# Sparse attention with an ELU feed-forward: 64-bit weights decoded in pairs of pieces, where they are staged

## The chip, the cores and the metric

One core of one Trainium2 chip. The metric is the time of one execution on the device in microseconds, the median of several runs. TensorE (PE) multiplies matrices, VectorE (DVE) and ScalarE (ACT) do the elementwise work, GpSimd (POOL) some of it and the indirect DMAs, and SyncE (SP) issues most other DMAs. Each engine takes its instructions in a fixed order.

## The reference, cut to what matters

```python
# q, k, v: (4, 8, 768, 64) float32; blocks of 32 tokens, 24 of them
mask = |blk_i - blk_j| <= 1, or block 0 or 23 on either side, or one of 3 sampled blocks per row block
attn = softmax(where(mask, q @ k^T / 8, -1e9)) @ v
x = attn, tokens by 512                     # 3072 x 512
h = x @ w_in                                # w_in 512 x 2048, float64
g = where(h > 0, h, exp(min(h, 0)) - 1)
out = g @ w_out                             # w_out 2048 x 512, float64
```

The two weight matrices come as 64-bit floats. No engine here computes in them: the kernel takes them as two 32-bit words each and builds a 32-bit float from sign, exponent and mantissa bits, which it then splits into two 16-bit floats (high part and rest). All products are made of three 16-bit products (high by high, high by low, low by high).

## The kernel before

**The work.** The 3072 tokens are 12 chunks of 256, three for each of the 4 batches. A chunk has two units of 128 query rows. For each unit and each half of the heads (qd): scores on TensorE (`scores`, L459), their minimum on VectorE (`sm_min`, L471), exp on ScalarE (`sm_exp`, L486), P split into two halves (`sm_hi` L493, `sm_lo` L498), turned by a DMA transpose (`sm_T`, L505; in chunk 0's first two units by TensorE, `turn_p`, L354), and multiplied with V (`attn_v`, L518). V rows are gathered from a scratch tensor in DRAM (`gather_v`, L416 and L418; `edge_v`, L408), after they have been split and stored there (`store_v`, L398). The first and last block of queries see all keys; `special` (sp, spt, spp, L554 to L605) handles them. The result is normed (`norm`, L538) and turned (`turn_x`, L332) into `xT`, the chunk's input of the feed-forward part.

**Feed-forward.** For each chunk, 8 tiles of h (`ffn_h`, L634; 24 matmuls of 128x256 each, into one of three PSUM tiles "f"), for each of them exp and relu on ScalarE (L642, L648), the minimum with h on VectorE (L652, "e<-h,e", which frees the PSUM tile), the high part of g (L656) and its rest (L659, on VectorE in chunk 0, else on GpSimd). Then two output tiles (`ffn_o`, L670, in four parts each), which need every g and every part of w_out. They are copied out by L678.

**The weights.** w_in and w_out are 16 pieces each, of 128x512 64-bit values (512 KB). `load_w` reads a piece into a room: the first three into the ring `wk` of three rooms, the next four into the tiles of g, which are not needed yet, all others into `wk` again, once its room is free. `w_bits1` works in place on ScalarE: the high word is scaled so that its exponent field becomes that of a 32-bit float (L245), and the top three bits of the low word's mantissa are made an integer (L247). `w_bits2` builds the float in a new tile of the ring "e" by two operations of VectorE, each with two sources: sign or low bits (L256), then the high word shifted by three, or that (L258). `w_split` makes the high part on ScalarE (L267) and the rest on VectorE (L268), in four dictionaries of tiles (`wih`, `wil`, `woh`, `wol`). So a piece takes three operations of ScalarE and three of VectorE, each of 512 columns. The ring "e" has four tiles and is shared with the outputs of `norm`, the e tiles of the feed-forward part and the output tiles r.

**The order.** `Steps` is a list of functions by step and rank; chunk t's h starts at step 12 + 16 t. Piece i gets its first bits at step 2 + 2i/3 and the rest a step later, so all 32 fall into chunk 0's part. `gate` holds the decoding of pieces 3 and on behind exps of the first units, and `more_w` (L836) holds four loads behind the first unit's last V rows. From the list, a scheduler makes each engine's order and the waits.

Of the kernel before, what the change touches and what calls it, by code (L numbers as in the profile page):

```python
# [39 lines left out]
def kernel(  # L40
# [198 lines left out]

    def w_bits1(i):  # L240


        s = wst[i]
        u = s.bitcast(F32)[:, :, 1]
        first = nc.scalar.activation(u, u, AF.Copy, scale=2.0 ** -111)  # L245

        nc.scalar.activation(  # L247
            s[:, :, 0], s.rearrange("p e w -> p (e w)").bitcast(U16).rearrange("p (e w) -> p e w", w=4)[:, :, 1],
            AF.Copy, scale=2.0 ** -13, bias=2.0 ** -14 - 0.5)
        return first  # L250

    def w_bits2(i):
        s = wst.pop(i)
        x = work.tile([P, 512], I32, tag="e", bufs=NE, name=f"wx{i}")
        wx[i] = x
        nc.vector.scalar_tensor_tensor(  # L256
            x, s[:, :, 1], -(2 ** 31), s[:, :, 0], op0=ALU.bitwise_and, op1=ALU.bitwise_or)
        nc.vector.scalar_tensor_tensor(  # L258
            x, s[:, :, 1], 3, x, op0=ALU.logical_shift_left, op1=ALU.bitwise_or)

    def w_split(i):
        hi, lo, nm = (wih, wil, "wi") if i < NFC else (woh, wol, "wo")
        f = i % NFC
        hi[f] = const.tile([P, 512], F16, tag=f"{nm}h{f}", name=f"{nm}h{f}")
        lo[f] = const.tile([P, 512], F16, tag=f"{nm}l{f}", name=f"{nm}l{f}")
        x = wx.pop(i).bitcast(F32)
        nc.scalar.activation(hi[f], x, AF.Copy)  # L267
        nc.vector.tensor_tensor(lo[f], x, hi[f], op=ALU.subtract)  # L268
# [354 lines left out]
    gh = [gg[f // 2][:, 0, f % 2] for f in range(NFP)]  # L623
    gl = [gg[f // 2][:, 1, f % 2] for f in range(NFP)]

    def ffn_h(t, f):
        ps = ps_f.tile([P, 2, CW], F32, tag="f", name=f"h{t}_{f}")
        x = xT[t]
        for e in range(2):
            n = 0  # L630
            for cc in range(NCC):
                cs = slice(cc * P, (cc + 1) * P)
                for w, l in ((wih, 0), (wih, 1), (wil, 0)):
                    nc.tensor.matmul(  # L634
                        ps[:, e, :], lhsT=w[2 * f + e][:, cs], rhs=x[:, l, cc, :],
# [26 lines left out]
    def ffn_o(t, m, part, nparts):  # L662
# [4 lines left out]
        for f in range(NFP * part // nparts, NFP * (part + 1) // nparts):  # L667
            for e in range(2):
                for n, (g, w) in enumerate(((gh, woh), (gh, wol), (gl, woh))):
                    nc.tensor.matmul(  # L670
                        o, lhsT=g[f][:, e, ms], rhs=w[2 * f + e],
# [236 lines left out]
```

## Time and profile before

| what | value |
|---|---|
| median of 3 runs | 772.99 us (768.12 to 774.59) |
| the profiled execution's own time | 768.26 us |
| its span, first to last instruction | 766.5 us |
| busy: PE, DVE, ACT, POOL | 683.3, 461.8, 407.0, 194.1 us |
| mean granted TensorE clock | 0.95 |

A row of a group reads: line, engine, operation, output<-inputs, shapes, count | busy us, mean ns of one | idle time of the engine ahead of it and what ended it. A row of the timeline: start us, duration us, engine, line, operation, count [idle time ahead <-what ended it]. "issue" is idle time without a cause that the profile shows; SPq, DVEq are an engine's queue. The trace has 32 pieces decoded between 21.8 and 169 us.

### The profile page before, as it was taken

The numbers are of one execution on the slowest core, as the hardware profiler recorded it, in microseconds if no ns is written. First come the engines' busy times: TensorE is split into PE (matmuls) and PEld (weight loads), VectorE is DVE, ScalarE is ACT, GpSimd is POOL, SyncE is SP. The second block draws the span as 40 slices with busy tenths as digits, with TensorE's granted clock in tenths as the row PEclk, the third lists the DMA queues.
The fourth block names the chain that finished last, engine by engine and source line by source line (L and its number), as shares of the span: only waits on it lengthen the run. The fifth ranks groups of instructions, "written<-read, shape, count | busy, mean of one in ns | idle before, by whom it ended". The sixth has DMA issues, their size and how long they took to land. (4 is left out here: it accounts for less than half of the span.)

```text
span 766.5 us, 30298 instructions
## 1 busy us (share of the span) xinstructions
PE 683.3 (89%) x12999; PEld 476.1 (62%) x12999; DVE 461.8 (60%) x1253; ACT 407.0 (53%) x880; POOL 194.1 (25%) x193
## 2 busy tenths in 40 slices
PE   1447568599889999999999999999999999999997
PEld 1336454247646857758658658668568577586673
DVE  3849899686856755845655846647467358354130
ACT  2558798664834746545535546536456355353240
POOL 1414002001521421512413303325205215222040
PEclk9757789789999999999999999999999999999999
DMA  9996867969969678775796567597595635531000
GB/s 206 312 278 184 248 195 170 215 137 233 210 136 176 154 160 160 184 150 98 167 186 155 132 179 142 140 181 147 114 189 136 112 58 139 127 68 33 29 1 28
DMA packets 205307, 116.34 MB, mean 152 GB/s; under 512 B 163316, under 2 KB 183924, under 8 KB 205172
## 3 DMA queue, kind: packets, MB, share of 16 engines
q1 hardware_dynamic: 192464, 89.41, 53.6%
q0 software_dynamic: 5824, 17.83, 8.8%
q10 hardware_dynamic: 6884, 7.15, 3.4%
q8 instruction: 102, 1.67, 0.9%
q14 instruction: 33, 0.27, 0.1%
HBM read 74.52 MB, written 12.58 MB: 114 GB/s over the span
## 5 line engine op out<-in xcount | busy, mean ns | idle before, releaser
L634 PE MATMUL h<-xT,wih 128*128 128x256 f16 x1536 | 259.7, 276 | 7.5 <-DVE e L652 7.5
L670 PE MATMUL o<-woh,g 128*128 128x512 f16 x768 | 240.3, 384 | 3.7 <-ACT woh L267 3.7
L634 PE MATMUL h<-xT,wil 128*128 128x256 f16 x768 | 211.2, 275 | 0.0
L670 PEld LDWEIGHTS <-g 128*128 128x128 f16 x1152 | 109.9, 99 | 128.9 <-issue 5.1
L659 POOL TENSOR_TENSOR g<-e,g 128x512 f16<-128x512 f32 x88 | 102.9, 1172 | 322.0 <-DVE g L656 294.7
L634 PEld LDWEIGHTS <-wih 128*128 128x128 f16 x1536 | 148.1, 99 | 29.3 <-issue 6.6
L670 PE MATMUL o<-wol,g 128*128 128x512 f16 x384 | 146.9, 383 | 0.0
L418 POOL DMA_INDIRECT vg<-scr,rix x88 | 84.9, 964 | 204.2 <-PE av L518 183.7
L486 ACT ACTIVATE t<-t,m 128x256 f32<-128x256 f32 x176 | 87.2, 496 | 72.2 <-DVE m L471 72.2
L652 DVE SCALAR_TENSOR_TENSOR e<-h,e 128x512 f32<-128x512 f32 x96 | 66.1, 689 | 54.4 <-ACT e L648 51.3
L642 ACT ACTIVATE e<-h 128x512 f32<-128x512 f32 x96 | 56.3, 587 | 51.6 <-PE h L634 49.6
L634 PEld LDWEIGHTS <-wil 128*128 128x128 f16 x768 | 75.9, 99 | 9.8 <-issue 0.4
L471 DVE CUSTOM_DVE_ANT_1 t<-s,mask 128x256 f32<-128x256 f32 x176 | 64.6, 419 | 18.8 <-PE s L459 18.8
L498 DVE SCALAR_TENSOR_TENSOR p<-t,p 128x1024 f16<-128x1024 f32 x40 | 48.7, 1218 | 37.2 <-ACT p L493 37.2
L648 ACT ACTIVATE e<-e,gs 128x512 f32<-128x512 f32 x96 | 69.3, 722 | 1.8
L459 PEld LDWEIGHTS <-qT 64*32 64x32 f16 x4224 | 41.5, 93 | 41.6 <-issue 33.1
L459 PE MATMUL s<-kT,qT 64*32 64x96 f16 x2112 | 45.1, 214 | 16.4 <-issue 7.4
L459 PE MATMUL s<-kR,qT 64*32 64x160 f16 x2112 | 48.8, 245 | 11.9 <-DVE kR L427 5.3
L518 PEld LDWEIGHTS <-pT 128*32 128x32 f16 x4224 | 41.3, 96 | 21.1 <-issue 12.0
L518 PE MATMUL av<-vg,pT 128*32 128x64 f16 x4224 | 47.7, 198 | 6.9 <-DMA pT<-p 4.7
L427 DVE COPY kR<-kT 128x256 f16 x246 | 46.3, 235 | 10.4 <-issue 6.6
L656 DVE CAST g<-e 128x512 f16<-128x512 f32 x96 | 48.8, 508 | 2.7
(101 smaller groups left out, 635.1 us busy)
## 6 DMA issues: line engine op xcount, KB each, us to landing
vg<-scr SPq DMA_DIRECT2D x88, 192.0 KB
wk<-in_moe_w_out_dram SPq DMA_DIRECT2D x16, 512.0 KB
wk<-in_moe_w_in_dram SPq DMA_DIRECT2D x12, 512.0 KB
scr<-vN SPq DMA_DIRECT2D x12, 512.0 KB
out_dram<-r ACTq DMA_DIRECT2D x20, 256.0 KB
stq<-in_q_dram SPq DMA_DIRECT2D x18, 256.0 KB
stv<-in_v_dram SPq DMA_DIRECT2D x18, 256.0 KB
stk<-in_k_dram SPq DMA_DIRECT2D x18, 256.0 KB
```

What stands on the lines that cost most here:

```text
L418: nc.gpsimd.indirect_dma_start(out=t[0:96, 1, i], out_offset=None, in_=scr[b], in_offset=bass.IndirectOffsetOnAxis(ap=rix[0:96, qb : qb + ...
L459: nc.tensor.matmul(ps[32 * n : 32 * n + 32, j, pp, c], lhsT=qT[b, u][js, ql, a, q0 : q0 + 32], rhs=m, start=(ql + kl + part == 0), stop=(q ...
L471: nc.vector.tensor_tensor_reduce(t[:, j, pp, :].rearrange("p (a b) -> p a b", b=BLOCK), ps[:, j, pp, :].rearrange("p (a b) -> p a b", b=BL ...
L486: exps[b, u, qd] = nc.scalar.activation(t[:, j, pp, :], t[:, j, pp, :], AF.Exp, bias=m[:, j, pp : pp + 1], scale=-1.0, accum_out=s[:, h : ...
L518: nc.tensor.matmul(o[32 * n : 32 * n + 32, 4 * qd + 2 * pp + j, :], lhsT=t[:, pl * 8 + (2 * j + pp) * 2 + ab, 32 * n : 32 * n + 32], rhs=v ...
L634: nc.tensor.matmul(ps[:, e, :], lhsT=w[2 * f + e][:, cs], rhs=x[:, l, cc, :], start=(n == 0), stop=(n == 3 * NCC - 1))
L642: nc.scalar.activation(e, hS[t, f], AF.Exp, scale=IH)
L648: nc.scalar.activation(e, e, AF.Relu, bias=gs_col, scale=-GS)
L652: nc.vector.scalar_tensor_tensor(e, hS.pop((t, f)), -IH * GS, e, op0=ALU.mult, op1=ALU.min)
L656: nc.vector.tensor_copy(gh[f], eS[t, f])
L659: (nc.gpsimd if t else nc.vector).tensor_tensor(gl[f], eS.pop((t, f)), gh[f], op=ALU.subtract)
L670: nc.tensor.matmul(o, lhsT=g[f][:, e, ms], rhs=w[2 * f + e], start=(f == 0 and e == 0 and n == 0), stop=(f == NFP - 1 and e == 1 and n == 2))
```

## The change

1. **Pairs.** A table `WORK` lists 18 units of work in place of 32 pieces: 14 pairs of pieces, then four single pieces, each with its room. A pair is loaded by one DMA of 1 MB (w_in then in runs of 2 KB instead of 1 KB) and decoded by operations of 1024 columns.
2. **In place.** The float is built in the staged words themselves, in the word that was the low one, so every other word of the room holds a weight. The tile of the ring "e" goes.
3. **Sign.** Instead of L256 with two sources, an operation with one source (`tensor_scalar`, AND on 16-bit halves) puts the sign bit beside the integer of three bits, which ScalarE now writes as 16 bits. Then the shift and OR, in place. So a pair takes three operations of ScalarE and three of VectorE, as a single piece did.
4. **Rooms.** The weights' final tiles become `wi` (8) and `wo` (4), those of g two instead of four. A pair of w_in is staged in `wk`, in tiles of `wo` that wait for their weights, or in tiles of g; later ones in `wo` or `wk`.
5. **Loads.** Two pairs are asked for ahead of everything, two behind the first unit's V rows, three behind the second's; the others at the earliest step at which their room's last user is done, at most four steps ahead.

In `ffn_h` and `ffn_o` only the names of the tiles change; the matmuls are the same in number, shape and order within a tile.

```diff
+    WORK = [(0, 2, "k0"), (2, 2, 0), (4, 2, 1), (6, 2, 2), (8, 2, 3), (10, 2, "g0"),
...
+            (24, 2, 3), (26, 2, "k0"), (28, 1, "k2"), (29, 1, "k0"), (30, 1, "k1"), (31, 1, "k2")]
+    WFIRST, WMORE, WLATER = 2, 4, 7
...
     def w_bits1(i):
         s = wst[i]
-        u = s.bitcast(F32)[:, :, 1]
-        first = nc.scalar.activation(u, u, AF.Copy, scale=2.0 ** -111)
+        u, h = s.bitcast(F32)[:, :, 1], halves(s)
+        nc.scalar.activation(u, u, AF.Copy, scale=2.0 ** -111)
         nc.scalar.activation(
-            s[:, :, 0], s.rearrange("p e w -> p (e w)").bitcast(U16).rearrange("p (e w) -> p e w", w=4)[:, :, 1],
-            AF.Copy, scale=2.0 ** -13, bias=2.0 ** -14 - 0.5)
-        return first
+            h[:, :, 0], h[:, :, 1], AF.Copy, scale=2.0 ** -13, bias=2.0 ** -14 - 0.5)
+        nc.vector.tensor_scalar(h[:, :, 1], h[:, :, 3], 1 << 15, None, op0=ALU.bitwise_and)
 
     def w_bits2(i):
-        s = wst.pop(i)
-        x = work.tile([P, 512], I32, tag="e", bufs=NE, name=f"wx{i}")
-        wx[i] = x
-        nc.vector.scalar_tensor_tensor(
-            x, s[:, :, 1], -(2 ** 31), s[:, :, 0], op0=ALU.bitwise_and, op1=ALU.bitwise_or)
+        s = wst[i]
         nc.vector.scalar_tensor_tensor(
-            x, s[:, :, 1], 3, x, op0=ALU.logical_shift_left, op1=ALU.bitwise_or)
+            s[:, :, 0], s[:, :, 1], 3, s[:, :, 0], op0=ALU.logical_shift_left, op1=ALU.bitwise_or)
...
     def w_split(i):
...
+        x = wst.pop(i).bitcast(F32)[:, :, 0]
...
+        nc.scalar.activation(hi, x, AF.Copy)
+        nc.vector.tensor_tensor(lo, x, hi, op=ALU.subtract)
...
+    st.at(1, 9, lambda: more_w(0, range(WFIRST, WMORE)))
+    st.at(2, 9, lambda: more_w(1, range(WMORE, WLATER)))
+    for i, s in enumerate(w_step):
+        if i >= WLATER:
+            last = max((e for e in range(i) if held(e) & held(i)), default=0)
+            st.at(max(w_step[last] + 1, s - 4), 1.9, lambda i=i: load_w(i))
```

The scheduler's orders move with it, up to chunk 1's first h; from there on TensorE's order is the same. Three places. First VectorE, around chunk 0's first L652 (`e_0`; L671 in the changed kernel). Before (wx, wil: decoding; p, t, m: attention of unit 4):

```order
L256 SCALAR_TENSOR_TENSOR wx_1372<-wk 128x512
L323 SCALAR_TENSOR_TENSOR qT_5_1612<-qt_5_1613,qT_5_1612 128x512
L258 SCALAR_TENSOR_TENSOR wx_1372<-wk,wx_1372 128x512
L498 SCALAR_TENSOR_TENSOR p_4_0_1666<-t_4_0_1601,p_4_0_1666 128x1024
L268 TENSOR_TENSOR wil_1376<-wx_1372,wih_1375 128x512
L256 SCALAR_TENSOR_TENSOR wx_1411<-wk 128x512
L256 SCALAR_TENSOR_TENSOR wx_1414<-wk 128x512
L258 SCALAR_TENSOR_TENSOR wx_1411<-wk,wx_1411 128x512
L258 SCALAR_TENSOR_TENSOR wx_1414<-wk,wx_1414 128x512
L471 ISA t_4_1_1814,m_4_1_1815<-s_4_1_1673,mask 128x256
L471 ISA m_4_1_1815 128x1
L652 SCALAR_TENSOR_TENSOR e_0_1450<-h_0_1379,e_0_1450 128x512
```

In the changed kernel (L271 the AND, L275 shift and OR, L288 the rest):

```order
L271 TENSOR_SCALAR wo_87<-wo_87 128x1024
L343 SCALAR_TENSOR_TENSOR qT_4_1283<-qt_4_1284,qT_4_1283 128x512
L275 SCALAR_TENSOR_TENSOR wo_87<-wo_87 128x1024
L271 TENSOR_SCALAR wo_88<-wo_88 128x1024
L275 SCALAR_TENSOR_TENSOR wo_88<-wo_88 128x1024
L288 TENSOR_TENSOR wi_86<-wo_87,wi_86 128x1024
L671 SCALAR_TENSOR_TENSOR e_0_1355<-h_0_1297,e_0_1355 128x512
L671 SCALAR_TENSOR_TENSOR e_1_1485<-h_1_1330,e_1_1485 128x512
L675 CAST g_91<-e_0_1355 128x512
L288 TENSOR_TENSOR wo_87<-wo_88,wo_87 128x1024
L678 TENSOR_TENSOR g_91<-e_0_1355,g_91 128x512
L675 CAST g_91<-e_1_1485 128x512
```

The first two L652 now stand behind the last pair of w_in and ahead of all minima of unit 4, where they stood behind the first of that unit's two halves. With them TensorE's h0_3 and h0_4 have moved ahead of that unit's second scores.

Second SP, around the first DMA transpose of chunk 1's unit 4. Before:

```order
L416 DMA vg_85<-scr_221 96x1024 x2
L233 DMA wk<-in_moe_w_in_dram 128x4x256
L295 DMA stk_0_2078<-in_k_dram 128x8x64
L233 DMA wk<-in_moe_w_in_dram 128x4x256
L237 DMA wk<-in_moe_w_out_dram 128x1024 x2
L505 DMA_TRANSPOSE pT_4_0_1770<-p_4_0_1666 128x16x128
L237 DMA wk<-in_moe_w_out_dram 128x1024 x8
L505 DMA_TRANSPOSE pT_4_1_1927<-p_4_1_1908 128x16x128
```

In the changed kernel:

```order
L436 DMA vg_94<-scr_230 96x1024
L255 DMA wo_89<-in_moe_w_out_dram 128x2x1024
L436 DMA vg_94<-scr_230 96x1024
L255 DMA wo_90<-in_moe_w_out_dram 128x2x1024
L436 DMA vg_94<-scr_230 96x1024
L255 DMA wk<-in_moe_w_out_dram 128x2x1024
L436 DMA vg_94<-scr_230 96x1024
L333 DMA stq_2_1361<-in_q_dram 128x8x64
L255 DMA wk<-in_moe_w_out_dram 128x1024
L320 DMA stv_0_0_1701<-in_v_dram 128x4x128
L436 DMA vg_95<-scr_230 96x1024
L525 DMA_TRANSPOSE pT_4_0_1650<-p_4_0_1547 128x16x128
```

Ahead of the transpose all of w_in and four pairs and a single piece of w_out are asked for, where it was two pieces of w_out; the loads of pairs 9 and 10 (into wo_89, wo_90) stand among the V gathers of unit 4.

Third ScalarE, around the exps of the special rows (spt_1). Before:

```order
L267 ACTIVATE woh_2119<-wx_2113 128x512
L247 ACTIVATE wk<-wk 128x512
L267 ACTIVATE woh_2123<-wx_2116 128x512
L245 ACTIVATE wk<-wk 128x512
L247 ACTIVATE wk<-wk 128x512
L572 ACTIVATE spt_1_0_2163,spm_1_0_2160<-sp_1_0_2081,spm_1_0_2160 128x768
```

In the changed kernel (L267 and L269 are the bits, L287 the high part):

```order
L287 ACTIVATE wo_89<-wo_90 128x1024
L267 ACTIVATE wk<-wk 128x512
L269 ACTIVATE wk<-wk 128x512
L602 ACTIVATE spp_0_1_1926<-spt_0_1_1785,spm_0_1_1782 128x768
L592 ACTIVATE spt_1_0_2006,spm_1_0_2003<-sp_1_0_1934,spm_1_0_2003 128x768
L287 ACTIVATE wo_89<-wk 128x1024
```

The bits that stand ahead of these exps are now of a single piece in the ring's third room, which no piece used before it; it is asked for ahead of the transpose in the SP order above.

More of the change, by code (lines that the diff above doesn't have):

```diff
@@ L212, in build_mask @@
         nc.scalar.activation(mask, pm, AF.Copy, scale=NEG * SS)
-    gg = [const.tile([P, 2, 2, 2, CW], F16, tag=f"g{i}", name=f"g{i}") for i in range(NFP // 2)]
-    wih, wil, woh, wol, wst = {}, {}, {}, {}, {}
-    wx = {}
+    wi = [const.tile([P, 2, NCC, 2, P], F16, tag=f"wi{f}", name=f"wi{f}") for f in range(NFP)]
+    wo = [const.tile([P, 2, 2, 2, 512], F16, tag=f"wo{m}", name=f"wo{m}") for m in range(NFP // 2)]
+    gt = [const.tile([P, 2, 2, 2, 2, CW], F16, tag=f"g{i}", name=f"g{i}") for i in range(NFP // 4)]
@@ new lines @@
+    WFIRST, WMORE, WLATER = 2, 4, 7
+    assert NFC == 16
+    wst = {}
+    def w_room(i):
+        n, room = WORK[i][1:]
+        if room == "k0" and n == 2:
+            return wk[:, 0:2].rearrange("p a e w -> p (a e) w")
+        if str(room)[0] == "k":
+            return wk[:, int(room[1])]
+        x = gt[int(room[1])] if str(room)[0] == "g" else wo[room]
+        x = x.rearrange("p a b c d e -> p (a b c d e)" if str(room)[0] == "g" else "p a b c d -> p (a b c d)")
+        return x.bitcast(I32).rearrange("p (e w) -> p e w", w=2)
@@ L261, in w_split @@
     def w_split(i):
[L262 to L268, printed above, removed]
+        f, n, _ = WORK[i]
+        x = wst.pop(i).bitcast(F32)[:, :, 0]
+        if f < NFC:
+            hi, lo = (wi[f // 2][:, l].rearrange("p c e f -> p (c e f)") for l in range(2))
+        else:
+            f -= NFC
+            hi, lo = (wo[f // 4][:, f // 2 % 2, l, f % 2 : f % 2 + n].rearrange("p e d -> p (e d)")
+                      for l in range(2))
@@ L631, in ffn_h @@
             for cc in range(NCC):
-                cs = slice(cc * P, (cc + 1) * P)
-                for w, l in ((wih, 0), (wih, 1), (wil, 0)):
+                for xl, wl in PROD_X:
                     nc.tensor.matmul(
-                        ps[:, e, :], lhsT=w[2 * f + e][:, cs], rhs=x[:, l, cc, :],
+                        ps[:, e, :], lhsT=wi[f][:, wl, cc, e, :], rhs=x[:, xl, cc, :],
                         start=(n == 0), stop=(n == 3 * NCC - 1))
```

53 lines of the change are left out of this document (26 added, 27 removed).

## The prediction

> **What bounds the kernel now.** I read the stages first: the trace cut at the places where the work changes character. The columns are the stage, its length, then busy time of each engine with its number of instructions, the clock granted to TensorE, and the share of the DMA engines.
>
> ```profile
> core 0: us, PE busy (x) PEld busy (x) DVE busy (x) ACT busy (x) POOL busy (x), PEclk, DMA share, GB/s
> 24.00:60.00 36.00, 15.93 (x583) 12.33 (x570) 21.73 (x77) 19.25 (x48) 11.21 (x12) 0.55 0.99 269
> 60.00:120.00 60.00, 36.48 (x734) 28.69 (x722) 55.05 (x102) 51.52 (x111) 8.47 (x8) 0.78 0.72 211
> 120.00:177.00 57.00, 45.65 (x890) 25.26 (x890) 46.86 (x122) 38.28 (x81) 6.96 (x6) 0.85 0.84 190
> 177.00:766.00 589.00, 576.79 (x10776) 403.13 (x10774) 327.57 (x913) 288.75 (x627) 164.09 (x154) 1.00 0.61 132
> ```
>
> From 177 us on TensorE is busy 576.8 of 589 us at full clock: nothing but TensorE matters there, and whatever the start of that stage gains, the end gains. Ahead of it TensorE idles a third of the time. From 60 to 120 the full engine is VectorE (55.05 of 60), with ScalarE behind it (51.52); from 24 to 60 no engine is full, but DMA is (0.99).
>
> Next, the timeline of TensorE between 80 and 180 us, its idle times and what ended them (in brackets).
>
> ```profile
> 88.66 0.28 PE L459 MATMUL s<-kT,qT 64*32 64x96 f16 x8 [5.67 <-DVE m L471]
> ...
> 99.41 0.23 PE L518 MATMUL av<-vg,pT 128*32 128x64 f16 x1 [4.68 <-DMA pT<-p]
> ...
> 109.35 0.38 PE L634 MATMUL h<-xT,wih 128*128 128x256 f16 x2 [1.82 <-DVE e L652]
> ...
> 120.00 0.37 PE L634 MATMUL h<-xT,wih 128*128 128x256 f16 x1 [3.27 <-DVE e L652]
> ...
> 139.40 0.90 PE L332 MATMUL qt<-ident,stq 128*128 128x128 f32 x3 [5.35 <-ACT spt L572]
> ...
> 151.06 0.58 PE L670 MATMUL o<-woh,g 128*128 128x512 f16 x1 [3.66 <-ACT woh L267]
> ...
> 176.82 0.39 PE L634 MATMUL h<-xT,wih 128*128 128x256 f16 x2
> ```
>
> Three of these waits are for a VectorE operation (the minimum of the scores, then L652, which frees the PSUM tile of h) that stood in a full queue among weight pieces; the last wait is for a weight piece itself. The row at 176.82 is chunk 1's first h: the start of the stage that TensorE bounds. So the price of the change is how much earlier this row comes.
>
> The wait at 139.40 has its root on ScalarE, which sat in front of a w_out piece that had not landed, with the exps of the special rows behind it:
>
> ```profile
> 137.28 0.65 ACT L245 ACTIVATE wk<-wk 128x512 f32<-128x512 f32 x1 [5.70 <-DMA wk<-in_moe_w_out_dram]
> ```
>
> **The change, part by part.** First the prices. Groups with their mean duration in ns (last number ahead of the second bar), the two ring groups and the like of what comes in their place:
>
> ```profile
> L256 DVE SCALAR_TENSOR_TENSOR wx<-wk 128x512 int32<-128x512 int32 x28 | 18.9, 689 | 1.4 <-ACT wk L247 1.4
> L258 DVE SCALAR_TENSOR_TENSOR wx<-wk,wx 128x512 int32<-128x512 int32 x28 | 18.9, 687 | 0.0
> L268 DVE TENSOR_TENSOR wil<-wx,wih 128x512 f16<-128x512 f32 x16 | 10.9, 688 | 1.9 <-ACT wih L267 1.8
> L323 DVE SCALAR_TENSOR_TENSOR pT<-pt,pT 128x1024 f16<-128x1024 f32 x4 | 4.9, 1223 | 2.8 <-ACT pT L320 2.8
> L656 DVE CAST g<-e 128x512 f16<-128x512 f32 x5 | 2.1, 425 | 0.0
> L427 DVE COPY kR<-kT 128x256 f16 x246 | 46.3, 235 | 10.4 <-issue 6.6 <-PE s L459 1.6 <-PE pt L354 0.3
> L579 DVE TENSOR_SCALAR spm<-spm 128x1 f32<-128x1 f32 x16 | 2.5, 154 | 12.1 <-ACT spt L572 12.1
> ```
>
> and how closely such operations follow each other (start times in the first column):
>
> ```profile
> 60.09 1.23 DVE L323 SCALAR_TENSOR_TENSOR pT<-pt,pT 128x1024 f16<-128x1024 f32 x1 [1.47 <-ACT pT L320]
> 61.23 0.68 DVE L538 TENSOR_TENSOR xf<-av,sum 128x512 f32<-128x512 f32 x1
> 61.83 1.28 DVE L256 SCALAR_TENSOR_TENSOR wx<-g 128x512 int32<-128x512 int32 x2
> ...
> 110.42 0.42 DVE L656 CAST g<-e 128x512 f16<-128x512 f32 x1
> 110.75 0.69 DVE L258 SCALAR_TENSOR_TENSOR wx<-wk,wx 128x512 int32<-128x512 int32 x1
> ```
> ```profile
> 54.33 0.64 ACT L245 ACTIVATE g<-g 128x512 f32<-128x512 f32 x1
> 54.87 0.64 ACT L247 ACTIVATE g<-g 128x512 int32<-128x512 uint16 x1
> ...
> 91.55 1.05 ACT L493 ACTIVATE p<-t 128x1024 f16<-128x1024 f32 x1
> 92.49 0.68 ACT L245 ACTIVATE wk<-wk 128x512 f32<-128x512 f32 x1
> ```
>
> From start to start a two-source operation of 512 columns costs VectorE 0.60 us (61.23 to 61.83), one of 1024 costs 1.14 (60.09 to 61.23). ScalarE: 0.54 for 512, 0.94 for 1024. The new operation, the AND with one source, 1024 columns of 16 bit at every fourth place, has no row. A one-column operation takes 154 ns; the cast, one source at full width, adds (425 - 154)/512 = 0.53 ns a column; the copy of short runs of 16 bit (235 - 154)/256 = 0.32; two sources (1223 - 154)/1024 = 1.04. So the AND lies between 0.48 and 1.22 us. I take the cast's slope: 0.70 us, 0.61 from start to start.
>
> A pair of pieces thus costs VectorE 6 x 0.60 = 3.60 us before and 0.61 + 1.14 + 1.14 = 2.89 after; ScalarE 6 x 0.54 = 3.24 before and 3 x 0.94 = 2.82 after.
>
> *Term 1, from 60 us to L652 of the fifth h tile (h0_4), minus 11 us.* This is where VectorE is full.
>
> ```profile
> 60.00:119.25 59.25, 13.47 (x20) 0.78 0.72 208
> ```
> ```profile
> 119.25 0.69 DVE L652 SCALAR_TENSOR_TENSOR e<-h,e 128x512 f32<-128x512 f32 x1
> ```
>
> The first row is L256 alone in this stretch: 20 pieces, and L258 and L268 go with it, so 60 operations, 36.0 us of 59.25. In the change's order the same L652 has pairs 0 to 10 and two thirds of pair 11 ahead of it. Pairs 0 to 2 stand ahead of the last turned P of the first units, so they run before 60, where VectorE had 14 us to spare (21.73 of 36): one and a half pairs more than before are covered there. What is left is 8 x 2.89 + 1.75 = 24.9 us: 11.1 less. ScalarE has to follow: by the order it has 23 operations of 0.94 ahead of that point, 21.6 us, against about 60 of 0.54, 32.4, so it gives the same 11. TensorE has room for it (23.5 us idle in 60 to 120), and by the order h0_3 and h0_4 now stand ahead of the scores that waited 5.67 us.
>
> *Term 2, from there to 176.82, minus 6.5 us.* Decoding left: 9 pieces of 1.80 before, 16.2 us; after, 1.14 for pair 11, two pairs (5.8) and four single pieces of about 1.54 (6.2), 13.1. VectorE is busy 46.86 of 57 there, so I count half of the 3.1: 1.5. The wait of 5.70 goes: the piece that now stands ahead of those exps is read into a room that is free from the start. Singles 29 to 31 still reload used rooms, so 5 of it are counted. Bounds: 0 (another wait takes over at once) to 9.
>
> *Term 3, before 60, plus 4 us.* SP's queue now carries two loads of 1 MB ahead of the stores of vN and the V gathers, 0.5 MB more: at 269 GB/s 1.9 us later. The first product with V did not wait for V but for ScalarE, so most of this is covered; uncovered it is the 1.9.
>
> ```profile
> 41.37 0.71 PE L518 MATMUL av<-vg,pT 128*32 128x64 f16 x32 [1.11 <-ACT pT L320]
> ```
> ```profile
> PE s L459 <- issue: 11.7, 3, 4.9
> ```
> ```profile
> 21.78 0.71 ACT L245 ACTIVATE wk<-wk 128x512 f32<-128x512 f32 x1
> ```
>
> The third row is ScalarE's first decoding, without a wait; in the change it needs the whole megabyte, up to 1.9 us later, and the last split of K and those of Q stand behind it. For these two: 1.5. The second row: TensorE waited 11.7 us, in three pieces, all between 33 and 57 us, for nothing that the profile shows, in the stage with DMA at 0.99. The change brings 2 MB more forward by 60 us, 7.4 us more of such traffic; at 11.7 us per 36 that is 2.4 (0 to 6.5, if it lasts to 80).
>
> SP gets new waits: the loads of pairs 9 and 10 wait for the rooms of pairs 3 and 4, and the gathers of V for the fifth unit stand between and behind them. Both rooms come free ahead of the first h in VectorE's order; these V rows are first read at 99.41, three h tiles later. The transpose of P that follows on SP waits for VectorE anyway. I count nothing; if that cover were gone, the product at 99.41 would start later by the lateness of the gathers, as it now does by 4.68 for the transpose.
>
> Edits that cost nothing: the layout of w and g (same shapes and counts of matmuls and of stores), loads of w_in in runs of twice the length, the ring "e" without the decoded words.
>
> Sum: 768.26 - 11 - 6.5 + 4 = 754.8 for an execution like the profiled one. That one lies 4.7 under the median of the runs, 772.99; the four executions known (768.12 to 774.59) have a mean of 771.0, 2.7 above it. Forecast: 757.5, rounded **757 us**.
>
> **The rivals.**
> *A: the AND runs at one column per cycle of a two-source operation*, 1.22 us. For it: its columns lie 8 bytes apart, and no one-source row here is like that. Against: the cast. Price 0.53 us for each of 8.7 pairs in term 1 and about 1.5 behind: 6 us. 763.
>
> *B: the load moves to the front.* DMA at 0.72 from 60 to 120 leaves 28%, but pairs 4 to 8 are asked for in a burst, and if TensorE's unexplained waits go on until 80 us (6.5), and the 3.4 of loads ahead are not covered, term 3 is 10. For it: three waits in the full stage. Against: VectorE decodes on during them. 763 to 764.
>
> *C, slower: the writes to every other word.* The changed kernel's AND and shift write into the staged words, 8 bytes apart; before, VectorE read so but wrote dense (L256, L258). If such a write took two cycles a column, both would cost about 2.2 us, a pair 5.5, and term 1 would be 8.3 x 5.5 + 1.75 - 36 = +11 and the tail +7 instead of minus 1.5: about 784. It decides from about 1.5 ns a column for both operations on (there a pair costs 4.2 and term 1 is nothing). Against: L256 takes two sources so spaced at 689 ns, as much as L268 with dense ones (688).
> [...]
>
> *D: the attention chain binds, not VectorE's sum.* The wait of 4.68 for a DMA transpose stays as it is; if minimum, exp, transpose and product set the pace between 80 and 177, less decoding changes nothing: 768 to 771. Against: two waits for L652 and one for the minimum in the rows above, behind decoding.
>
> **How the numbers follow.** Main case 0.58 (745 to 764), A 0.10, B 0.18, C 0.06, D 0.08. Low end: the AND at 0.48 (3 us), term 2 at 9 and term 3 at 0: 745 after rounding. High end 770: D still in, C out. A measurement here tells about 1%, 7.7 us: below 763 is faster. Main 0.57, A 0.07, B 0.10 make 0.74; 0.18 within; slower is C and 0.02 of D, 0.08.
>
> **What would show it.** The AND near 0.70 us, the shift near 1.22; VectorE's time on decoding down from 66 us (96 operations of 0.69) to about 51; the fifth L652 at about 110 instead of 119.25; no wait for w_out ahead of the exps of the special rows; chunk 1's first h at about 163 instead of 176.82, and from there on the same length. Wrong: the AND or the shift above 1.5 us (C), waits on issue after 60 us (B), or an early fifth L652 and yet a late first h of chunk 1 (D).

## The result and the profile after

| kernel | median us | runs | ratio to before, 95% interval |
|---|---|---|---|
| before | 769.49 | 16 | |
| changed | 774.97 (772.15 to 780.92) | 16 | 1.0063 (1.0039 to 1.0087) |

The change makes the kernel slower by 0.6%, where 757 us were forecast and 770 was the high end of the range. Some executions on one of the chips used below ran in a slower state; medians and ratios in this document leave them out. The profiled execution of the changed kernel has a span of 774.2 us. Line numbers of the changed kernel: L267 scales the high word, L269 makes the low bits, L271 is the AND, L275 the shift, L287 and L288 split; L653 is h, L671 the minimum that frees its PSUM tile, L689 the output product.

The stages first, cut as before:

```profile
core 0: us, PE busy (x) PEld busy (x) DVE busy (x) ACT busy (x) POOL busy (x), PEclk, DMA share, GB/s
24.00:60.00 36.00, 14.30 (x501) 10.96 (x502) 25.86 (x73) 23.32 (x41) 12.07 (x12) 0.53 1.03 303
60.00:120.00 60.00, 38.37 (x759) 30.30 (x757) 47.55 (x68) 58.03 (x79) 10.47 (x8) 0.73 0.58 179
120.00:177.00 57.00, 45.96 (x830) 25.09 (x830) 49.00 (x122) 45.14 (x82) 7.48 (x6) 0.87 0.84 203
```

Between 60 and 120 us VectorE is relieved (47.55, it was 55.05), but ScalarE is now the full engine: 58.03 of 60, it was 51.52. The groups of the decoding say why (here the nine pairs that are staged in tiles of `wo`):

```profile
L269 ACT ACTIVATE wo<-wo 128x1024 uint16<-128x1024 uint16 x9 | 22.4, 2494 | 0.0
L271 DVE TENSOR_SCALAR wo<-wo 128x1024 uint16<-128x1024 uint16 x9 | 12.0, 1329 | 6.9 <-ACT wo L269 6.9
L275 DVE SCALAR_TENSOR_TENSOR wo<-wo 128x1024 int32<-128x1024 int32 x9 | 11.0, 1220 | 0.1
L267 ACT ACTIVATE wo<-wo 128x1024 f32<-128x1024 f32 x9 | 10.3, 1144 | 0.0
```

The operation that makes the low bits takes 2.49 us, its neighbour L267 of the same width 1.14. The AND takes 1.33, more than the 1.22 that bounded it in the prediction, and ahead of these ANDs VectorE waits 6.9 us for L269. The timeline of TensorE at the places that were read before:

```profile
78.16 0.80 PE L653 MATMUL h<-xT,wi 128*128 128x256 f16 x3 [0.83 <-ACT xT L340]
...
98.44 1.87 PE L653 MATMUL h<-xT,wi 128*128 128x256 f16 x8 [4.97 <-DVE e L671]
...
129.50 0.88 PE L574 MATMUL sp<-kT,qT 64*64 64x512 f16 x6 [2.83 <-ACT spt L592]
...
177.92 2.25 PE L653 MATMUL h<-xT,wi 128*128 128x256 f16 x19
```

The first h of all starts at 78.16 (71.74 before), that of chunk 1 at 177.92 (176.82 before). In another execution of the same kernel (a0 below) chunk 1's first h starts at 182.91, so differences of up to 5 us at this row between single executions say little. The fifth L671, forecast for 110, starts at 121.37 (120.76 in a0):

```profile
121.37 0.68 DVE L671 SCALAR_TENSOR_TENSOR e<-h,e 128x512 f32<-128x512 f32 x1
```

### The profile page after: what moved, and what is told of

Read it like the earlier page. It is cut to its first block, busy times and chain, and to the rows that moved or that the text cites. A ratio compares the mean times of both kernels' runs of the same rounds, so it can differ in the third digit from the quotient of the medians.

```text
span 774.2 us, 30186 instructions
## 1 busy us (share of the span) xinstructions
PE 687.7 (89%) x12999; PEld 478.3 (62%) x12999; DVE 461.5 (60%) x1211; ACT 423.4 (55%) x838; POOL 197.2 (25%) x193
## 3 DMA queue, kind: packets, MB, share of 16 engines
q10 hardware_dynamic: 6884, 7.15, 3.4%
## 5 line engine op out<-in xcount | busy, mean ns | idle before, releaser
L653 PE MATMUL h<-xT,wi 128*128 128x256 f16 x2304 | 268.9, 278 | 9.3 <-DVE e L671 7.8
L689 PE MATMUL o<-wo,g 128*128 128x512 f16 x1152 | 262.6, 382 | 0.7 <-DVE wo L288 0.5
L653 PEld LDWEIGHTS <-wi 128*128 128x128 f16 x2304 | 225.5, 99 | 43.1 <-issue 9.1
L689 PEld LDWEIGHTS <-g 128*128 128x128 f16 x1152 | 109.2, 98 | 128.4 <-issue 4.0
L438 POOL DMA_INDIRECT vg<-scr,rix x88 | 87.8, 997 | 200.3 <-PE av L538 179.8
L671 DVE SCALAR_TENSOR_TENSOR e<-h,e 128x512 f32<-128x512 f32 x96 | 65.8, 688 | 53.1 <-ACT e L667 50.1
L661 ACT ACTIVATE e<-h 128x512 f32<-128x512 f32 x96 | 56.6, 589 | 53.7 <-PE h L653 49.5
L447 DVE COPY kR<-kT 128x256 f16 x246 | 47.9, 243 | 12.6 <-issue 7.4
L697 ACT ACTIVATE r<-o 128x512 f32<-128x512 f32 x24 | 14.3, 594 | 52.5 <-PE o L689 52.5
L513 ACT ACTIVATE p<-t 128x1024 f16<-128x1024 f32 x40 | 42.2, 1055 | 1.1
L343 DVE SCALAR_TENSOR_TENSOR xT<-xt,xT 128x512 f16<-128x512 f32 (+1 forms) x28 | 16.1, 576 | 39.3 <-ACT xT L340 39.3
```

Source lines behind the costliest of these rows:

```text
L438: nc.gpsimd.indirect_dma_start(out=t[0:96, 1, i], out_offset=None, in_=scr[b], in_offset=bass.IndirectOffsetOnAxis(ap=rix[0:96, qb : qb + ...
L653: nc.tensor.matmul(ps[:, e, :], lhsT=wi[f][:, wl, cc, e, :], rhs=x[:, xl, cc, :], start=(n == 0), stop=(n == 3 * NCC - 1))
L661: nc.scalar.activation(e, hS[t, f], AF.Exp, scale=IH)
L671: nc.vector.scalar_tensor_tensor(e, hS.pop((t, f)), -IH * GS, e, op0=ALU.mult, op1=ALU.min)
L689: nc.tensor.matmul(o, lhsT=g[f][:, e, ms], rhs=wo[f // 2][:, f % 2, l, e], start=(f == 0 and e == 0 and n == 0), stop=(f == NFP - 1 and e ...
```

## The experiments

Theory W: the 16-bit write of ScalarE is the loss. Rivals: the loads in front (L), VectorE's sum and the AND (V, A), later the shared ring "e" (R). The runs fell on several chips: on most the kernel before takes about 770 us, on one 802 to 804. So each kernel is given with its ratio to before on its own chip, five rounds each; equal times of before stand for the same chip. The ratio with its interval can differ by 0.25% from the quotient of the two medians, so differences of 2 or 3 us are not told by these runs.

| kernel | median us | before there | ratio, 95% interval |
|---|---|---|---|
| e1: low bits written as 32 bits | 789.90 | 804.05 | 0.9829 (0.9798 to 0.9860) |
| e2: and sign by two sources | 795.43 | 804.05 | 0.9889 (0.9852 to 0.9927) |
| e3: before, new operations alone | 802.15 | 804.05 | 0.9992 (0.9958 to 1.0027) |
| a0: the changed kernel again | 773.66 | 770.08 | 1.0041 (1.0013 to 1.0069) |
| e1 again | 762.11 | 770.08 | 0.9921 (0.9880 to 0.9962) |
| e5: e1 with a 32-bit AND | 761.47 | 770.08 | 0.9881 (0.9835 to 0.9926) |
| e6: 32-bit AND, 16-bit low bits | 773.91 | 770.08 | 1.0046 (1.0015 to 1.0077) |
| e7: e1, pairs done in halves | 762.47 | 770.31 | 0.9879 (0.9849 to 0.9909) |
| e8: e1, loads later | 768.49 | 770.31 | 0.9962 (0.9932 to 0.9992) |
| e9: e5 without the low bits | 760.07 | 770.31 | 0.9856 (0.9819 to 0.9892) |
| e10: before without the low bits | 770.62 | 770.31 | 1.0013 (0.9986 to 1.0039) |
| e11: before, in place | 799.05 | 802.41 | 0.9978 (0.9941 to 1.0016) |
| e12: rooms alone | 801.25 | 802.41 | 0.9983 (0.9934 to 1.0031) |
| e12 again | 766.38 | 770.25 | 0.9952 (0.9930 to 0.9973) |
| e14: before, short loads | 797.26 | 802.41 | 0.9960 (0.9920 to 1.0000) |
| e15: rooms and in place, old operations | 761.74 | 770.25 | 0.9886 (0.9846 to 0.9926) |

### The two new operations, with the order unchanged

e1 is the changed kernel with one output widened:

```diff
-            h[:, :, 0], h[:, :, 1], AF.Copy, scale=2.0 ** -13, bias=2.0 ** -14 - 0.5)
+            s[:, :, 0], h[:, :, 1], AF.Copy, scale=2.0 ** -13, bias=2.0 ** -14 - 0.5)
```

e5 is e1, and e6 the changed kernel, with the AND on whole words:

```diff
-        nc.vector.tensor_scalar(h[:, :, 1], h[:, :, 3], 1 << 15, None, op0=ALU.bitwise_and)
+        nc.vector.tensor_scalar(s[:, :, 0], s[:, :, 1], -(2 ** 31), None, op0=ALU.bitwise_and)
```

On every engine the instructions of these kernels stand in the same order as in the changed kernel, so beside the two operations' durations nothing was changed.

> The changed kernel with one operation undone: ScalarE writes the three low bits as a 32-bit integer, as before, and the AND overwrites its upper half. Every engine's order is that of the changed kernel. Theory W (ScalarE's write of 16 bits at every fourth place is the whole loss): the operation falls from 2.48 us to about 1.15 per 1024 columns, ScalarE is busy some 47 of the 60 us from 60 to 120 instead of 58, and the time falls by 8 to 14 us, to 761 to 767. Rival L (the earlier loads and TensorE's waits on issue take the gain, or the attention chain binds): the operation gets as cheap, but the time falls by less than 4 us, to 771 or more.

> The changed kernel itself, beside the three that follow: all four have the same order of instructions on every engine and differ only in what two operations write. Here ScalarE's low bits are written as 16 bits (2.48 us per 1024 columns) and the AND as 16 bits (1.32 us). Theory W: 1.006 of before again, and 12 to 18 us above the kernel with 32-bit low bits. Rival L (the size of that gain came from the other chip, not from the operation): within 5 us of it.

> Low bits as 32-bit integers, AND as 16 bits, once more on the chip of the three others. Theory W: 0.983 of before again. Rival L: within 5 us of the changed kernel.

> Low bits as 32-bit integers, and the AND as one of 32 bits with one source (0.70 us per 1024 columns in the run of single operations, the price that the prediction took), written over the low word. It leaves out the three low bits of each weight, which this AND overwrites; ScalarE still makes them. VectorE gets 14 x 0.62 + 4 x 0.3, about 10 us, less to do. Theory V (VectorE's sum is what sets the pace from 60 to 177 us, as the prediction's first term has it): 4 to 8 us below the kernel with the 16-bit AND. Rival O (what counts is ScalarE and the order and the early loads; VectorE's sum no longer binds): within 2 us of it.

> The cheap AND, but ScalarE writes 16 bits as in the changed kernel; again the three low bits are left out. Theory W: ScalarE (58 of 60 us from 60 to 120) holds it, so it stays within 3 us of the changed kernel although VectorE has 10 us less to do. Rival A (the AND at 1.32 in place of 0.70 is a large part of the loss): 5 us or more below the changed kernel.

On one chip: 773.66 and 773.91 with the 16-bit low bits, 762.11 and 761.47 with the 32-bit ones. ScalarE's write is worth 11.6 to 12.4 us by these medians (9 to 13 by the ratios). Theory W holds. Beside the dear write the cheap AND is worth nothing (773.66 and 773.91), so A falls for the changed kernel. Theory V is not borne out, but not excluded either: in e5 VectorE has some 10 us less to do than in e1 (14 pairs at 1.33 - 0.70, four single pieces at 0.75 - 0.42), and the time falls by 0.6 us by the medians, by 3 by the ratios, within their intervals, where V wanted 4 to 8. The same piece of ScalarE's timeline, first of the changed kernel, then of e1 (second run):

```profile
86.60 1.17 ACT L267 ACTIVATE wo<-wo 128x1024 f32<-128x1024 f32 x1
87.65 2.48 ACT L269 ACTIVATE wo<-wo 128x1024 uint16<-128x1024 uint16 x1
89.87 0.69 ACT L340 ACTIVATE qT<-qt 128x512 f16<-128x512 f32 x1
90.44 1.17 ACT L267 ACTIVATE wo<-wo 128x1024 f32<-128x1024 f32 x1
91.49 2.55 ACT L269 ACTIVATE wo<-wo 128x1024 uint16<-128x1024 uint16 x1
93.75 0.72 ACT L661 ACTIVATE e<-h 128x512 f32<-128x512 f32 x1
```

```profile
83.48 1.16 ACT L267 ACTIVATE wo<-wo 128x1024 f32<-128x1024 f32 x1
84.55 1.09 ACT L269 ACTIVATE wo<-wo 128x1024 int32<-128x1024 uint16 x1
85.54 0.57 ACT L340 ACTIVATE qT<-qt 128x512 f16<-128x512 f32 x1
86.02 1.15 ACT L267 ACTIVATE wo<-wo 128x1024 f32<-128x1024 f32 x1
87.07 1.15 ACT L269 ACTIVATE wo<-wo 128x1024 int32<-128x1024 uint16 x1
88.11 0.57 ACT L661 ACTIVATE e<-h 128x512 f32<-128x512 f32 x1
```

L661, the last row, is the first operation on chunk 0's first h, whose PSUM tile TensorE waits for. From the first L267 it is reached after 7.15 us in the one and after 4.63 in the other. Over the stage from 60 to 120 us L269 alone takes, in the changed kernel and in e1:

```profile
60.00:120.00 60.00, 22.53 (x9) 0.73 0.58 179
```

```profile
60.00:120.00 60.00, 11.34 (x10) 0.74 0.69 209
```

The 11.2 us between them are, within a microsecond, the time that e1 gains. That the two agree so closely is in part chance: over the whole kernel L269 takes 22 us less in e1, and of the 10.9 us between the two profiled executions 7.4 are there at chunk 1's first h and the others come behind it.

> The one before, and the AND with one source replaced by the operation with two sources, on pairs and in place (sign, or low bits). Theory W: the AND took 1.32 us, the two-source operation takes about 1.22, so VectorE gains 1.4 us over 14 pairs and the time is within 2 us of the run before it. Rival V (the AND is a large part of the loss, as it stands ahead of the shift on VectorE): 4 us or more below the run before it.

```diff
-        nc.vector.tensor_scalar(h[:, :, 1], h[:, :, 3], 1 << 15, None, op0=ALU.bitwise_and)
+        nc.vector.scalar_tensor_tensor(
+            s[:, :, 0], s[:, :, 1], -(2 ** 31), s[:, :, 0], op0=ALU.bitwise_and, op1=ALU.bitwise_or)
```

e2, here against the changed kernel. It came out 0.6% above e1, neither of the two expectations; but the scheduler put several operations elsewhere, so this says nothing on the AND itself.

### What it is about the write

Two kernels of single operations, on tiles filled with ones.

> Only the operations in question, six of each, 1024 columns, on tiles filled with ones; the kernel computes nothing else and writes zeros. ScalarE, theory W (a 2-byte write at a step is what costs): 2.4 us for each write of 16 bits at every second or fourth place, in place or into another tile, about 1.1 for 16 bits written densely and for 32 bits at any step, whatever is read. Rival P (reading and writing the same word in place costs): 2.4 in place only, 1.1 into another tile. Rival R (the read of 16 bits at every fourth place costs as well): above 1.5 for a dense write too. VectorE: 1.3 us for the AND at every fourth place; theory W: dense to dense about 0.6 or less; if the write is what costs, reading at every fourth place into a dense row is cheap as well; if the read is, reading at every fourth place stays at 1.3 with a dense output.

> Single operations, four of each, 1024 columns from dense 32-bit words; nothing else is computed and zeros are written out. ScalarE writes 16-bit floats densely, at a step of 4 bytes, at a step of 8, then two side by side in every 8 bytes, then 32-bit floats at a step of 8; then VectorE the same with two equal sources. If the type of the data plays no part: ScalarE about 1.1, 1.4, 2.4 us, then between 1.1 and 1.4, then 1.1; VectorE with two sources about 1.2 for all but the step of 8, where the 16-bit write costs 1.3 or more. If the 2.5 us was due to the conversion to integers, floats cost 1.1 at every step.

From the first, ScalarE with 16-bit output at every fourth place, in place (s) and into another tile (d); with a dense source; and with 32-bit output at every second word:

```profile
23.34 2.52 ACT L35 ACTIVATE d<-s 128x1024 uint16<-128x1024 uint16 x1
25.61 2.52 ACT L35 ACTIVATE s<-s 128x1024 uint16<-128x1024 uint16 x1
...
53.78 4.97 ACT L35 ACTIVATE d<-s 128x1024 uint16<-128x1024 uint16 x2
...
67.01 6.75 ACT L35 ACTIVATE s<-s 128x1024 int32<-128x1024 uint16 x6
```

Starts follow each other by 2.27 us in the first two rows, 2.5 in the third, 1.13 in the last. From the second kernel, ScalarE with 16-bit floats at a step of 8 bytes, then two side by side in every 8 bytes, then 32-bit floats at a step of 8:

```profile
14.98 4.97 ACT L48 ACTIVATE d<-s 128x1024 f16<-128x1024 f32 x2
...
25.00 4.32 ACT L50 ACTIVATE d<-s 128x1024 f16<-128x1024 f32 x4
29.34 4.56 ACT L52 ACTIVATE d<-s 128x1024 f32<-128x1024 f32 x4
```

In microseconds from start to start, 1024 columns:

| output | ScalarE | VectorE, one source | VectorE, two sources |
|---|---|---|---|
| 16 bit, dense | 1.09 | 0.46 | 1.26 |
| 16 bit, two side by side in every 8 bytes | 1.09 | | 1.26 |
| 16 bit, every 4 bytes | 1.37 | 0.77 | 1.33 |
| 16 bit, every 8 bytes, dense source | 2.50 | 1.33 | 2.47 |
| 16 bit, every 8 bytes, source at every 8 bytes | 2.26 | 1.13 | |
| 16 bit dense, source at every 8 bytes | 1.14 | 0.73 | |
| 32 bit, every 8 bytes | 1.13 to 1.15 | 0.73 | 1.26 |

In the fifth row the outputs s and d take turns, and an operation starts about 0.25 us before the last one ends (2.52 long, 2.27 apart in the rows above). Where one tile was written again and again, the next started only behind the last (two in 4.97 from 53.78 on, so 2.47 long and 2.50 apart). The durations hardly differ (2.52 and 2.47), so the spaced source is not what makes that row shorter.

So on ScalarE it is the write, not the read, the place or the conversion: a lone 16-bit value in every 8 bytes costs 2.3 times a dense one (2.50 against 1.09), 32 bits in the same place next to nothing extra (1.13 to 1.15). On VectorE it costs 2.0 times with two sources (2.47 against 1.26) and 2.9 times with one (1.33 against 0.46), where reading so costs something as well (0.73 against 0.46). The rivals P and R of the first of these runs fall; theory W's 2.4 for a step of 4 bytes was too much (1.37).

### Where the forms cost nothing

> The kernel before with the new operations alone: single pieces, its rooms and loads, but ScalarE writes 16 bits, the AND has one source, and one shift-and-or writes the ring. Theory W: ScalarE's operation goes from 0.66 to about 1.35 us per piece, 22 us in all, some 14 of them between 60 and 120 us where ScalarE was already busy 51.5 of 60; 8 to 14 us slower than before. Rival L: ScalarE has the room, the forms cost nothing, within 3 us of before.

> The kernel before without ScalarE's operation for the three low bits; the sign operation keeps two sources, both the high word, so VectorE's time is the same and the three low bits are left out. ScalarE has 21 us less to do. Theory S (in the kernel before ScalarE waits for loads and for VectorE, so its time is covered, which is why 22 us more cost nothing there): within 3 us of before. Rival: ScalarE counts there as well, 5 us or more below before.

```diff
# e3, the kernel before with
+            h[:, :, 0], h[:, :, 1], AF.Copy, scale=2.0 ** -13, bias=2.0 ** -14 - 0.5)
+        nc.vector.tensor_scalar(h[:, :, 1], h[:, :, 3], 1 << 15, None, op0=ALU.bitwise_and)
-            x, s[:, :, 1], 3, x, op0=ALU.logical_shift_left, op1=ALU.bitwise_or)
+            x, s[:, :, 1], 3, s[:, :, 0], op0=ALU.logical_shift_left, op1=ALU.bitwise_or)
# e10, the kernel before without L247, and
-            x, s[:, :, 1], -(2 ** 31), s[:, :, 0], op0=ALU.bitwise_and, op1=ALU.bitwise_or)
+            x, s[:, :, 1], -(2 ** 31), s[:, :, 1], op0=ALU.bitwise_and, op1=ALU.bitwise_and)
```

e3 puts the new operations into the kernel before, still single pieces in the ring. ScalarE pays 1341 instead of 662 ns per piece, 22 us in all, and the time is the same (0.9992): theory W's 8 to 14 us were wrong here. e10 goes the other way, 21 us less on ScalarE, and again the time is the same. The group of the first decoding operation shows what gave way. The kernel before, then e10, then e3 (its profile is from the chip of 802 to 804 us), then the changed kernel, whose first pair alone waited:

```profile
L245 ACT ACTIVATE wk<-wk 128x512 f32<-128x512 f32 x28 | 18.9, 674 | 15.4 <-DMA wk<-in_moe_w_out_dram 11.5 <-DMA wk<-in_moe_w_in_dram 3.9
```

```profile
L245 ACT ACTIVATE wk<-wk 128x512 f32<-128x512 f32 x28 | 18.8, 677 | 19.9 <-DMA wk<-in_moe_w_out_dram 14.2 <-DMA wk<-in_moe_w_in_dram 5.7
```

```profile
L250 ACT ACTIVATE wk<-wk 128x512 uint16<-128x512 uint16 x28 | 37.6, 1341 | 0.0
L248 ACT ACTIVATE wk<-wk 128x512 f32<-128x512 f32 x28 | 19.2, 684 | 4.5 <-DMA wk<-in_moe_w_out_dram 2.9 <-DMA wk<-in_moe_w_in_dram 1.6
```

```profile
L267 ACT ACTIVATE wk<-wk 128x1024 f32<-128x1024 f32 x3 | 3.4, 1145 | 1.0 <-DMA wk<-in_moe_w_in_dram 1.0
```

In the kernel before, ScalarE's work fills time in which it would wait for pieces: 15.4 us of waiting as it is, 4.5 with more work, 19.9 with less. In the changed kernel pieces are there early, L267 waits 1.0 us in all, and ScalarE has nothing to hide the dear write behind. What covers the other half of e3's 22 us was not traced.

### Where the remaining gain comes from

> The pairs undone in the operations alone: rooms, loads, in-place build and 32-bit low bits as in the best run so far (762.1 where before is 770.1, ratio 0.992), but each operation on a pair is done as two of 512 columns. From start to start ScalarE pays 0.54 x 2 instead of 0.94, 5.9 us in all, VectorE 0.60 x 2 instead of 1.14, 2.5 us. Theory S (the gain is early loads and order, the pairs only save these 6 and 3 us): 2 to 4 us above the kernel with pairs. Rival P (the pairs are the gain): 6 us or more above it, at before or over.

> The kernel with the 32-bit AND, without ScalarE's operation for the three low bits, which that AND overwrote; the three low bits stay left out. ScalarE has 19 us less to do, some 10 of them between 60 and 120. Theory S (ScalarE sets the pace there, 57 of 60 us busy, which is why the cheap AND gained nothing): 4 to 9 us below the kernel with the operation, ratio to before about 0.98. Rival D (VectorE or the attention chain binds by now): within 3 us of it, ratio about 0.988.

> The kernel with pairs and 32-bit low bits, but only one pair asked for behind the first unit's V rows and two behind the second's, the others at their step, where it was two and three. Rival B of the prediction (the early megabytes cost TensorE waits on issue): 3 us or more below the kernel with the early loads, and fewer such waits between 60 and 75 us. Theory L (early loads are what the change gains by, since decoding doesn't wait for them): 3 us or more above it, with ScalarE waiting for pieces. Neither: within 3 us.

```diff
# e7, e1 with every operation of w_bits1, w_bits2 and w_split in a loop
+        for s in parts(wst[i]):
# e9, e5 with
-        nc.scalar.activation(
-            s[:, :, 0], h[:, :, 1], AF.Copy, scale=2.0 ** -13, bias=2.0 ** -14 - 0.5)
# e8, e1 with
-    WFIRST, WMORE, WLATER = 2, 4, 7
+    WFIRST, WMORE, WLATER = 2, 3, 5
```

e7 splits each operation of e1 into two and loses nothing (762.47). e9 takes another 19 us from e5's ScalarE. From 60 to 120 us, e5 and then e9:

```profile
60.00:120.00 60.00, 44.25 (x792) 33.68 (x784) 52.26 (x85) 57.13 (x98) 9.79 (x8) 0.86 0.82 230
```

```profile
60.00:120.00 60.00, 45.92 (x824) 34.26 (x827) 54.45 (x89) 50.00 (x91) 7.94 (x8) 0.81 0.83 229
```

ScalarE falls from 57.13 to 50.00 and the time by 1.4 us only (1.9 by the ratios, on two chips). So with the dear write gone neither sum alone decides much: 10 us less on VectorE (e1 to e5) and 19 less on ScalarE (e5 to e9) each gave a microsecond or two at the end, not clear of the noise. e8 is 6 us slower than e1, and than e7 on its own chip, but the sixth pair's load jumped to third place in SP's queue there, so it mixes two things. The first h of all and that of chunk 1 in e1 (second run):

```profile
76.10 0.81 PE L653 MATMUL h<-xT,wi 128*128 128x256 f16 x3
...
170.56 2.79 PE L653 MATMUL h<-xT,wi 128*128 128x256 f16 x24
```

In e8 they start at 73.95 and 175.78, the one earlier and the other later: the placing of loads can be worth microseconds, in which direction these runs don't tell.

Left were rooms with early loads, and the build in place, which takes the weights out of the ring "e". In e11, e12 and e15 all operations are the old ones, on single pieces:

> The kernel before with one part of the change: each piece is built in its staged words, in place, so the ring of four tiles that is shared with the outputs of the attention and the feed-forward part is free of weights; single pieces, two-source sign, rooms and loads as before. Theory L (what is left of the gain, 8 us, comes from rooms and early loads): within 3 us of before. Theory R (the shared ring held decoding back): 4 to 8 us faster than before.

> The other way round: rooms, loads and tiles of the change, but every piece decoded singly, with the old operations (32-bit low bits, sign with two sources) into the shared ring of four tiles. Theory L: still 6 to 10 us faster than before, ratio 0.987 to 0.993, as with pairs and in place. Theory R: within 3 us of before.

> The kernel before, where each piece after the seventh is loaded with an eighth of its columns; the rest of the room holds old data, so most weights are left out and the output is not the reference's. Operations are the same in number and size; the scheduler lets decoding come up to a few places earlier. ScalarE waits 15.4 us for pieces in the kernel before. Theory L: these waits go and the time falls by 5 to 10 us. Rival: they were covered, within 3 us of before.

> Rooms, loads and tiles of the change and the build in place, with all the old operations: single pieces, 32-bit low bits, sign with two sources. It differs from the next run in one thing alone, where the float is built. Theory J (rooms with early loads and the freed ring gain only together, each alone is held by the other): ratio to before 0.983 to 0.991, 5 us or more below the next run. Rival N (the gain needs the new sign operation or the pairs): within 3 us of the next run.

> Rooms, loads and tiles of the change with the old operations, the float built in the shared ring of four tiles, beside the run in place on the same chip. Theory J: 0.995 to 1.002 of before. Rival N: the same as the run in place.

```diff
# e11, the kernel before with
-        x = work.tile([P, 512], I32, tag="e", bufs=NE, name=f"wx{i}")
+        x = s[:, :, 0]
# e15, e7 with the sign by two sources, in place, for the AND
+                s[:, :, 0], s[:, :, 1], -(2 ** 31), s[:, :, 0], op0=ALU.bitwise_and, op1=ALU.bitwise_or)
# e12, e15 with both operations of VectorE writing
+            x = work.tile([P, 512], I32, tag="e", bufs=NE, name=f"wx{i}_{a}")
# e14, the kernel before, pieces after the seventh (w_out; w_in likewise)
-                s.rearrange("p e w -> p (e w)"), w_out.bitcast(I32)[f * P : (f + 1) * P, :])
+            eng.dma_start(s.rearrange("p e w -> p (e w)")[:, 0 : 1024 // n], w_out.bitcast(I32)[f * P : (f + 1) * P, 0 : 1024 // n])
```

In place alone: 0.9978, within the noise, on the chip of 802 to 804 us only. Rooms alone: 0.9983 and 0.9952. Both: 0.9886, and 4.6 us below rooms alone on the same chip, a little less than the 5 expected. Together they give 1.1%, more than the single ratios add up to (0.4 to 0.7%), though the intervals would allow the sum. TensorE's fourth h and the first L652 (L682 and L677 here), in e12 (second run) and in e15:

```profile
95.91 4.45 PE L664 MATMUL h<-xT,wi 128*128 128x256 f16 x20 [8.48 <-DVE e L682]
```

```profile
95.16 1.30 DVE L682 SCALAR_TENSOR_TENSOR e<-h,e 128x512 f32<-128x512 f32 x2
```

```profile
90.93 4.32 PE L659 MATMUL h<-xT,wi 128*128 128x256 f16 x23 [3.31 <-DVE e L677]
```

```profile
90.20 0.68 DVE L677 SCALAR_TENSOR_TENSOR e<-h,e 128x512 f32<-128x512 f32 x1
```

With the ring shared, the e tile of the first h comes 5.0 us later, and TensorE's fourth h waits 8.48 us instead of 3.31. That the tiles of the ring were what it waited for, and not the scheduler's other order, fits this but was not shown apart. e14 stayed between its two expectations by its ratio (0.9960, about 3 us; 5 by the medians): ScalarE still waited 10.8 us for pieces, where it was 15.4, so the waits that it was to remove were removed in part only.

## Why the prediction was wrong

**The step that failed** is the price of a pair on ScalarE, "3 x 0.94 = 2.82 after". It took the three operations as equal, by one dense row. One of them had its output changed from 32 bits to 16 bits at every 8 bytes, and the change's text said so. Measured from start to start, a pair costs 1.05 + 2.22 (the rows above) + 1.0 (L287), about 4.3 us: more than the 3.24 before. The 23 operations that the prediction had ahead of the fifth L671 then cost ScalarE 33 us, not 21.6, against 32.4 before: the 11 us that term 1 wanted from ScalarE are not there. With the low bits at 32 bits (e1) the kernel takes 11.6 us less, so this is the larger part of the 18 us between 774.97 and 757.

**The AND, 0.70 us**: 1.33, above the upper bound of 1.22. The bound came from a two-source row with a dense output (L323), and no row of before had a 16-bit output so spaced. Rival A put 6 us on it; by the medians e6 gives 0 and e5 0.6 (3 by the ratios). The 32-bit AND takes the 0.70 (690 ns in e5).

**Rival C** named writes to every other word. For 32-bit words it is wrong: the shift, which writes there, takes 1.22 us, as L323 does with a dense output (1223 ns). (Its own numbers, plus 11 and plus 7, make 788 and not "about 784", unless the tail is counted half.) What did decide is its neighbour, a write of half a word, and on ScalarE (L269 2.49 us, 1.12 with 32 bits in e1), for which no rival was worked out.

**Term 1, minus 11**, was to come from VectorE's shorter sum. With the prediction's own prices (e5) the fifth L671 does come early:

```profile
109.13 0.69 DVE L671 SCALAR_TENSOR_TENSOR e<-h,e 128x512 f32<-128x512 f32 x1
```

forecast was 110. With the AND at 1.33 (e1, second run) it comes 4.9 us later, about what rival A's price for term 1 gives (0.53 for each of 8.7 pairs). In e15 every piece costs VectorE its three old operations, as before, and the row still comes 6 us earlier than the 119.25 of before:

```profile
114.06 0.69 DVE L671 SCALAR_TENSOR_TENSOR e<-h,e 128x512 f32<-128x512 f32 x1
```

```profile
113.21 0.68 DVE L677 SCALAR_TENSOR_TENSOR e<-h,e 128x512 f32<-128x512 f32 x1
```

So the row obeys VectorE's sum in part, but as much came without shorter decoding: order, early pieces and the freed ring are left for it. And the end hardly follows the row: e1 and e5 differ by 0.6 us in their medians, and e15 is as fast as e5. The sign of rival D, an early fifth row and a late first h of chunk 1, is there in e5, weakly (166.59, where about 163 was forecast). The edit that the prediction costed at nothing, "the ring 'e' without the decoded words", is worth 4.6 us beside the rooms, together with the order that the scheduler then makes.

**Term 2, minus 6.5**: the 5.70 us wait for w_out on ScalarE is gone, as forecast: among ScalarE's waits from 60 to 177 us in the changed kernel none is for a piece.

**Term 3, plus 4**: the first h of all, in the kernel before and in e5:

```profile
71.74 1.10 PE L634 MATMUL h<-xT,wih 128*128 128x256 f16 x4
```

```profile
74.18 0.80 PE L653 MATMUL h<-xT,wi 128*128 128x256 f16 x3 [0.20 <-ACT xT L340]
...
166.59 2.79 PE L653 MATMUL h<-xT,wi 128*128 128x256 f16 x24
```

It came 2.4 us later in e5, 4.4 in e1, 6.4 in the changed kernel, where waits on issue went on after 60 us:

```profile
63.86 0.69 PE L538 MATMUL av<-vg,pT 128*32 128x64 f16 x37 [2.06 <-issue]
...
70.51 1.73 PE L538 MATMUL av<-vg,pT 128*32 128x64 f16 x114 [2.58 <-issue]
```

So rival B was right in part.

**"From there on the same length"** was wrong by some microseconds. From chunk 1's first h to the end the changed kernel takes 774.2 - 177.92 = 596.3 us (596.1 in a0), before 589.7; e5 593.6, from 166.59 on (the last row of e5 above). The first 75 us of it, in the changed kernel and in the kernel before:

```profile
177.92:252.92 75.00, 68.26 (x1211) 47.86 (x1204) 45.49 (x116) 35.97 (x77) 18.27 (x18) 0.95 0.76 165
```

```profile
176.82:251.82 75.00, 69.48 (x1341) 50.10 (x1333) 48.02 (x132) 38.81 (x84) 21.95 (x21) 1.00 0.87 181
```

The granted clock is 0.95, full in the kernel before, and TensorE idles 6.7 us, 1.2 more. Rooms and the build in place are not the cause: in e15, which has both with the old operations, the clock of these 75 us is full and the stretch to the end takes 590.0 us, while e7 has 0.93 and 595.4. What lowers the clock in the changed kernel and those close to it was not shown.

Put together, e5 is the kernel that the prediction had in mind: 761.47, inside the range (745 to 770) and 4.5 above its 757. That it comes so close is in part luck: e15 reaches 761.74 without the shorter sum on VectorE from which the prediction took most of its gain. The best kernels here that leave nothing out, e1, e7 and e15, lie at 762 on the chips of 770, 0.8 to 1.2% below before.

## What to carry to other kernels

When an edit changes the type or the spacing of an output, that operation needs a price of its own, on each engine that writes so; a lone 16-bit value in every 8 bytes cost two to three times a dense one here (2.50 against 1.09 us on ScalarE), and writing the whole 32-bit word and overwriting its half later was cheaper (1.12 against 2.49 us for L269; 762.11 against 773.66 in all, e1 and a0). Price every engine's share of a change in the stage where it has the least room: the same 22 us on ScalarE were free where it waited for loads, and cost about 12 where the other parts of the change had taken these waits away. A ring that two stages share may hide the gain of early loads (shown here by the times of e12 and e15, 766.38 and 761.74, not by the wait itself): test such parts singly and together.

## What the runs showed that was not expected

A one-source AND on 32-bit words at every second word takes VectorE 0.70 us for 1024 columns (690 ns in e5), while on 16-bit halves at every 8 bytes it takes 1.33 (1327 ns in e1). On one chip the same kernel took about 4.3% longer (802 to 804 against 770), and its profiles show TensorE waiting for issue in the late stage too, on the score products 11.9 to 14.7 us between 300 and 700 us of e2, e3, e11, e12 and e14, where the kernel before on another chip has none; the ratios of e1 (0.983 there, 0.992 on the other) differ by more than their intervals, so a chip can change the worth of an edit.
